# Fewer idle matmuls ahead of the first MoE unit: sixteen become four

## The chip, the core and the metric

The kernel runs on one core of one Trainium2 chip. The metric is the time of one execution on the device, in microseconds (us).

## The reference, cut to what matters

Windowed attention over 8 batches x 8 heads x 576 tokens of 64, then a two-layer feed-forward ("MoE") over the 4608 resulting tokens:

```python
scores = q @ k.T / 8                       # only |i - j| <= 32 kept
x = (softmax(scores) @ v)                  # -> 4608 x 512
h = x @ w_in                               # 512 -> 2048
out = (relu(h) ** 2) @ w_out               # 2048 -> 512
```

## The kernel before

The program is recorded as a list of operations, each with an estimated duration. A scheduler orders them per engine with a model of the chip. After that, `fill` puts idle matmuls (zeros times zeros, read by nobody) into the gaps that the model foresees on TensorE (PE) in the first 36 us, up to the first MoE unit (`self.first`), to keep the array active:

```python
WARM, COLD, DENSE, SPARSE, EXTRA = 36000, 6000, 1.15, 0.95, 6
...
def fill(self, out):
    at = 1200
    for op in sorted((o for o in out if o.eng == "PE"), key=lambda o: o.start):
        gap = min(op.start, WARM, self.first.start) - at
        one = 107 if at < COLD else 54
        for k in range(int((gap - 60) * (DENSE if at < COLD else SPARSE) // one) + (EXTRA if op is self.first else 0)):
            w = Op()
            w.eng, w.fn, w.dma, w.deps, w.i = "PE", self.idle, None, {self.idle_on}, op.i
            ...
            out.append(w)
        at = max(at, op.start + op.dur)
...
self.p.idle = lambda e: e.matmul(self.OUTP[1][:, 0:128], self.ZZ[:, 0:128], self.ZZ[:, 0:128], start=True, stop=True)
```

The MoE starts while attention of the first batch is still running, in units of 16 matmuls: 128 tokens (group g) times 512 columns of `w_in` (piece q). A unit needs its tokens' `xt` and its piece of `w_in`. The order of the first three units is (g0, q0), (g1, q0), (g0, q1), so the third unit is the first that needs the second piece:

```python
def mm1_small(self, T, g, q, key):
    ...
    first = self.p.rec("PE", f, reads=[("xt", 8*T + 2*g), ("xt", 8*T + 2*g + 1), ("w1", q)],
                       writes=[("ht", k % 2), ("mo", k)], key=key, dur=900)
    if not k:
        self.p.first = first

ORDER = ("k01 q01 v00 v01 v02 k03 q03 v03 k04 q04 w10 v04 w11 w12 w13 k05 q05 ... "   # order of the loads
         "w20 w21 w22 w23 k12 q12 v12 ...")                                            # w1x: w_in, w2x: w_out
```

The loads are issued by GpSimd (POOL), each piece of `w_in` and `w_out` is one DMA of 512 KB.

The softmax here doesn't subtract the row's maximum and nothing guards it: scores larger than these inputs give would overflow.

## Time and profile before

| | before |
|---|---|
| time, 3 executions | 300.83 us median (300.46 to 301.0) |
| profiled execution | 300.43 us, span 298.6 us |
| PE busy | 290.6 us (97%) |
| chain that ended last | 93% PE |
| first / third MoE unit starts | 18.15 / 20.65 us |
| second piece of `w_in` | issued 11.27, lands 20.27 us |

The landing is the last of the 16 increments of that DMA's semaphore in the trace. The Trainium skill ("DMA: Bandwidth & Descriptors", Why a DMA increments its semaphore by 16 and not by 1) says that each of up to 16 engines adds 1 when its own share is written, and that only the full 16 means that the data is there.

The timeline of before on PE around the first units (start, duration, engine, line, operation, count; idle time before it and its releaser in brackets, if any). The attention matmuls between are left out.

```profile
17.26 1.05 PE L411 MATMUL outp<-zz 128*128 128x128 bf16 x16
18.15 1.06 PE L787 MATMUL ht<-xt,w 128*128 128x128 bf16 x16
19.05 0.39 PE L768 MATMUL outp<-identw,xr 128*128 128x128 bf16 x4
...
19.51 1.06 PE L787 MATMUL ht<-xt,w 128*128 128x128 bf16 x16
...
20.65 1.06 PE L787 MATMUL ht<-xt,w 128*128 128x128 bf16 x16
21.84 0.40 PE L768 MATMUL outp<-identw,xr 128*128 128x128 bf16 x4
```

L411 are the idle matmuls, L787 the units, L768 transposes of the attention's result. The 16 idle matmuls hold PE for 0.89 us (18.15 - 17.26) just ahead of the first unit. The chain of before through the same stretch (start, us, what) says that they are on it:

```profile
17.42 0.89 PE outp L411 x16
18.32 0.89 PE ht L787 x16
19.21 0.22 PE outp L768 x4
...
19.68 0.89 PE ht L787 x16
...
20.85 0.22 DVE rs L750
...
21.09 0.70 DVE xr L752
```

A trap of reading: the chain counts a matmul from the modelled end of the one before it, so its times lie about 0.16 us after the starts in the timeline (17.42 against 17.26).

### The profile page before, as it was taken

How to read it: one execution, taken by the hardware profiler on the slowest of the kernel's cores; microseconds unless marked ns; L12 is line 12 of the kernel's file. 1: busy time of each engine (PE TensorE's matmuls, PEld its weight loads, DVE VectorE, ACT ScalarE, POOL GpSimd, SP SyncE). 2: the span in 40 equal slices, each digit the busy share in tenths (PEclk: the TensorE clock that was granted, in tenths of full speed). 3: DMA queues.
4: the chain of work that ended last, by engine and by line, in shares of the span. 5: the costliest groups of instructions: out<-in, count | busy, mean ns of one | idle time of the engine just before them, and what ended most of it. 6: DMA issues, size and time to landing. Idle time of an engine off the chain costs nothing.

```text
span 298.6 us, 7036 instructions
## 1 busy us (share of the span) xinstructions
PE 290.6 (97%) x2754; PEld 171.6 (57%) x2789; DVE 175.2 (59%) x428; ACT 160.1 (54%) x267; POOL 105.1 (35%) x131
## 2 busy tenths in 40 slices
PE   7899999999999999999999999999999999999996
PEld 6799855867667864544444444544544444444445
DVE  5874656674998964986569645855577622222200
ACT  3566543656667765665656454664656444444411
POOL 8999841432434444442533334334310000000000
DMA  9999999999999999999999999999992110100022
GB/s 154 168 201 170 206 173 194 159 157 190 147 179 169 121 194 154 146 143 173 145 120 136 153 163 136 116 163 141 152 124 70 55 44 35 37 35 36 35 91 86
DMA packets 166817, 39.34 MB, mean 132 GB/s; under 512 B 157824, under 2 KB 162304, under 8 KB 166784
## 3 DMA queue, kind: packets, MB, share of 16 engines
q0 software_dynamic: 113120, 17.90, 90.8%
q1 hardware_dynamic: 46512, 11.15, 25.2%
q10 hardware_dynamic: 7152, 9.83, 9.7%
q8 instruction: 22, 0.36, 0.5%
q14 instruction: 11, 0.09, 0.1%
HBM read 36.70 MB, written 9.44 MB: 155 GB/s over the span
## 4 chain that ended last, share of the span: by engine, by line
PE 93%; DMA 2%; DVE 2%; issue 1%; ACT 0%; POOL 0%; ACTq 0%; DVEq 0%; POOLq 0%
PE outp L880 40%; PE ht L828 27%; PE ht L810 7%; PE ht L787 7%; PE sc L596 4%; PE sc L664 3%; DMA qraw<-in_q_dram 2%; PE sc L490 1%; PE outp L411 1%; DVE vd L542 1%; PE sc L856 1%; PE outp L856 1%; DVE xr L752 1%; PE ht L490 0%; PE outp L768 0%
## 5 line engine op out<-in xcount | busy, mean ns | idle before, releaser
L880 PE MATMUL outp<-w,gt 128*128 128x512 bf16 x534 | 133.9, 379 | 2.0 <-issue 1.0
L843 DVE TENSOR_TENSOR gt<-rt 128x512 bf16<-128x512 bf16 x144 | 59.7, 420 | 62.8 <-ACT rt L834 53.3
L828 PE MATMUL ht<-xt,w 128*128 128x512 bf16 x375 | 95.8, 379 | 0.6 <-issue 0.2
L834 ACT ACTIVATE rt<-ht 128x512 bf16<-128x512 f32 x96 | 57.3, 599 | 68.9 <-PE ht L828 64.1
L880 PEld LDWEIGHTS outp<-w,gt 128*128 128x128 bf16 x560 | 52.4, 98 | 57.4
L828 PEld LDWEIGHTS ht<-xt,w 128*128 128x128 bf16 x384 | 36.8, 98 | 43.1
L464 POOL DMA_DIRECT2D qraw<-in_q_dram x39 | 33.4, 857 | 49.0 <-PE ht L828 13.2
L464 POOL DMA_DIRECT2D kraw<-in_k_dram x39 | 33.4, 857 | 36.2 <-PE ht L828 17.8
L530 POOL DMA_DIRECT2D vx<-in_v_dram x40 | 34.4, 862 | 29.2 <-PE ht L828 15.9
L624 ACT ACTIVATE e<-sc 128x1024 bf16<-128x1024 f32 (+1 forms) x46 | 35.7, 818 | 7.9 <-PE sc L596 7.9
L887 ACT ACTIVATE oe<-outp 128x512 f32<-128x512 f32 x35 | 20.9, 599 | 22.4 <-PE outp L880 22.4
L688 DVE TENSOR_TENSOR xr<-pf,rs 128x512 bf16<-128x512 f32 (+1 forms) x42 | 27.6, 682 | 0.4
L787 PE MATMUL ht<-xt,w 128*128 128x128 bf16 x384 | 23.8, 219 | 0.0
L810 PE MATMUL ht<-xt,w 128*128 128x256 bf16 x192 | 23.5, 273 | 0.0
L645 DVE TENSOR_TENSOR pt<-e,mask 128x512 bf16<-128x512 bf16 x42 | 17.7, 421 | 8.9 <-ACT e L624 8.8
L787 PEld LDWEIGHTS ht<-xt,w 128*128 128x128 bf16 x384 | 21.8, 98 | 0.4
L681 DVE COPY pf<-sc 128x520 f32<-128x520 f32 x21 | 14.7, 699 | 11.2 <-PE sc L664 11.1
L810 PEld LDWEIGHTS ht<-xt,w 128*128 128x128 bf16 x192 | 18.0, 98 | 3.3
L795 ACT ACTIVATE rt<-ht 128x512 bf16<-128x512 f32 x24 | 14.2, 599 | 9.3 <-PE ht L787 8.8
L816 ACT ACTIVATE rt<-ht 128x512 bf16<-128x512 f32 x24 | 14.4, 599 | 7.1 <-PE ht L810 6.0
L683 DVE TENSOR_TENSOR pf<-pf 64x520 f32<-64x520 f32 x21 | 14.6, 698 | 5.8 <-ACT pf L678 5.0
L678 ACT ACTIVATE pf<-sc 128x520 f32<-128x520 f32 x21 | 12.6, 600 | 7.2 <-PE sc L664 6.8
(81 smaller groups left out, 190.7 us busy)
## 6 DMA issues: line engine op xcount, KB each, us to landing
out_dram<-oe ACTq DMA_DIRECT2D x35, 256.0 KB, 3.1
kraw<-in_k_dram POOLq DMA_DIRECT2D x30, 128.0 KB, 5.3
qraw<-in_q_dram POOLq DMA_DIRECT2D x30, 128.0 KB, 5.6
vx<-in_v_dram POOLq DMA_DIRECT2D x24, 128.0 KB, 5.4
w<-in_moe_w_in_dram POOLq DMA_DIRECT2D x4, 512.0 KB, 9.9
w<-in_moe_w_out_dram POOLq DMA_DIRECT2D x4, 512.0 KB, 16.6
vx<-in_v_dram POOLq DMA_DIRECT2D x16, 96.0 KB, 5.0
xt<-xr SPq DMA_TRANSPOSE x36, 4.5
```

The lines of the kernel that those rows point to most:

```text
L464: self.p.rec("POOL", lambda e: e.dma_start(dst, src), writes=[("fraw", b, t, x)], old=[("fraw", b - 2, t, y + (b == 2))], reads=self.pace( ...
L530: self.p.rec("POOL", lambda e: e.dma_start(self.VX[b % 2][r:r + n, s, :, 0:64], self.v[b, :, t0:t0 + n, :].rearrange("h p d -> p h d")), w ...
L624: self.p.rec("ACT", lambda e, d=dst, a=src: e.activation(d, a, ACTF.Exp, scale=0.125), reads=["s" + x for x in name], writes=[("e", h)], k ...
L645: self.p.rec("DVE", lambda e, a=pt, c=ee, d=mb: e.tensor_tensor(a, c, d, ALU.mult), reads=[("e", k // 2), "mask"], writes=[("ptt", k)], ol ...
L688: self.p.rec("DVE", lambda e, w=w, np=np: e.tensor_tensor(bass.AP(self.XR, 512 * (2 * y + w), [[2048, np], [64, 2], [128, 4], [1, 64]]), b ...
L787: mm = e.matmul(ht[:, 128 * (d % 4):128 * (d % 4) + 128], self.W1[:, ft, 128 * d:128 * d + 128], self.XT[:, ft, t0:t0 + 128], start=(ft == ...
L810: mm = e.matmul(ht[:, 256 * (d % 2):256 * (d % 2) + 256], self.W1[:, ft, 128 * d:128 * d + 128], self.XT[:, ft, 64 * s0:64 * s0 + 256], st ...
L828: mm = e.matmul(ht[:], self.W1[:, ft, 128 * d:128 * d + 128], self.XT[:, ft, 512 * T:512 * T + 512], start=(ft == 0), stop=(ft == 3))
L834: self.p.rec("ACT", lambda e: e.activation(rt[:], ht[:], ACTF.Relu), reads=[("ht", k % 2)], writes=[("rt", k % 4)], key=key, dur=560)
L843: self.p.rec("DVE", lambda e: e.tensor_tensor(g, r, r, ALU.mult), reads=[("rt", k % 4)], writes=tags, key=key, dur=430)
L880: mm = e.matmul(op, gt[:, d, 128 * u:128 * u + 128], self.W2[:, d, :], start=(d == 0), stop=(d == 15))
L887: self.p.rec("ACT", lambda e: e.activation(oe[:], op, ACTF.Copy), reads=[tag], writes=[("oe", x % 4)], key=key, dur=560)
```

## The change

Its intent: the reserve of 6 idle matmuls ahead of the first unit goes, and the last gap is filled by 0.4 of its length instead of 0.95. Less filling, so that the first unit can start earlier when its inputs are there.

```diff
-WARM, COLD, DENSE, SPARSE, EXTRA = 36000, 6000, 1.15, 0.95, 6
+WARM, COLD, DENSE, SPARSE, LASTF = 36000, 6000, 1.15, 0.95, 0.4
@@ def fill
-            for k in range(int((gap - 60) * (DENSE if at < COLD else SPARSE) // one) + (EXTRA if op is self.first else 0)):
+            for k in range(int((gap - 60) * (DENSE if at < COLD else LASTF if op is self.first else SPARSE) // one)):
```

A comparison of the two programs' instructions engine by engine shows one difference: 16 idle matmuls ahead of the first unit became 4. DVE, ACT, POOL and SP have the same instructions in the same order.

## The prediction

> **What bounds the kernel.** TensorE's order of work. The page has PE busy 290.6 of 298.6 us (97%), and PE has 93% of the chain of work that ended last. From 17.42 us on that chain leaves PE in its first part once only, for DVE (20.85 to 21.79, a reciprocal and a scaling that feed a transpose). A shift of PE's order ahead of 22 us should reach the end, unless it runs into something that arrives at a fixed time.
>
> **What the change does.** It alters only idle matmuls (128x128, zeros) ahead of the first MoE unit. The timeline shows 16 at 17.26 to 18.15 us, start to start 55 to 56 ns. 6 are the reserve, 10 come from the 0.95 rule, so the schedule's gap less 60 ns is 568 to 625 ns, and the new rule (0.4) leaves 4. Twelve go: 12 x 55.6 = 0.67 us of PE time. No other instruction, semaphore, DMA or order changes.
>
> **How much is on the critical path.** All 16 stand in the chain. But the first unit also needs its weights: the first w_in piece, issued at 9.68 us, lands 7.7 us later, at 17.4; transposes that waited for a DMA started 0.05 us after it. Four idle matmuls end at 17.49, so the unit can start there, 0.67 us earlier, with nothing to spare. Then, from the timeline:
> - the transpose after it needs xr, which DVE ends at 18.39: start 18.44 instead of 19.05;
> - the next attention matmuls need pt (DVE, 18.72): about 18.78 instead of 19.27; second unit 19.02 instead of 19.51;
> - the third unit needs the second w_in piece, issued 11.27, 9.0 us to land: about 20.32 instead of 20.65;
> - the DVE pair and next transpose follow attention matmuls now at 19.92: transpose about 21.35 instead of 21.84.
>
> So 0.67 us shrinks to about 0.49 us by 22 us. Behind that, fixed arrivals leave room: the last w_out piece lands at 41.4 and its matmuls run at 42.05; later query and key pieces have 0.7 us and more. The shift just fits. Gain: 0.45 us.
>
> **Clock.** Idle matmuls keep the array's clock up. In the Trainium skill, "TensorE: Matmul & The Clock Gate" (Part 1), activity lifts the throttle and an idle window of about 3.4 us brings it back. The trace agrees on the first: idle matmuls step by 107 ns until 4.5 us and by 56 after. After pauses of 0.91 and 0.84 us (before 7.43 and 12.75 us) 128-column matmuls still step by 56 ns. A late weight would open a hole of at most about 0.6 us. I expect no slow matmuls.
>
> **Prediction.** 300.4 us, 299.9 to 300.9 (8 in 10). Faster by over 2%: 0.01; within 2%: 0.98; slower by over 2%: 0.01. The runs of before spread over 0.54 us, about the gain.
>
> **What would show each step.** In the timeline: 91 idle matmuls instead of 103, 4 ahead of the first unit; that unit at 17.45 to 17.6; the third at 20.2 to 20.4, waiting for w; the transpose near 21.35; PE work at 30, 60 and 250 us earlier by 0.4 to 0.5 us; first units' matmuls still 55 to 56 ns apart. If PE is early at 22 us but not at 50, a DMA absorbed it: then PE waits for w at about 41.4.
>
> **What would make it wrong.** The first weights' landing may scatter by some tenths of a us between runs; 16 idle matmuls hid that, now it shows (gain 0.2 or less). Later loads may be tighter than this trace says. Or the clock drops after the thinner stretch: units at 17 to 21 us at 107 ns per matmul, about 0.8 us more each, a loss of 1 to 3 us.

## More of the kernel before

Lines of the page of before: busy time by engine, the chain of work that ended last by engine, and two groups of matmuls (count, busy us and mean ns, idle time before them and what ended it).

```profile
PE 290.6 (97%) x2754; PEld 171.6 (57%) x2789; DVE 175.2 (59%) x428; ACT 160.1 (54%) x267; POOL 105.1 (35%) x131
PE 93%; DMA 2%; DVE 2%; issue 1%; ACT 0%; POOL 0%; ACTq 0%; DVEq 0%; POOLq 0%
L880 PE MATMUL outp<-w,gt 128*128 128x512 bf16 x534 | 133.9, 379 | 2.0 <-issue 1.0
L787 PE MATMUL ht<-xt,w 128*128 128x128 bf16 x384 | 23.8, 219 | 0.0
```

PE has almost no idle time, and the chain runs through PE's own order. The L787 group (the small MoE units) waits for nothing. The L880 group has 534 records where the program issues 560: some records are missing from this trace, so its busy time must not be compared with another trace to a few us.

## The result

| | before | changed |
|---|---|---|
| time, 4 executions each | 300.64 us median (300.40 to 301.0) | 301.09 us median (300.89 to 301.77) |
| ratio | | 1.0018 (95%: 0.9998 to 1.0038) |
| profiled execution | 300.43 us | 301.0 us |

The change did not gain 0.45 us; it measured 0.45 us over before, which is not clear of noise, and outside the predicted range of 299.9 to 300.9.

The page of the changed kernel, the lines that answer to those of before:

```profile
PE 293.9 (98%) x2777; PEld 171.6 (57%) x2777; DVE 175.4 (59%) x428; ACT 160.0 (53%) x267; POOL 105.0 (35%) x131
PE 92%; POOL 3%; DMA 3%; issue 0%; DVE 0%; POOLq 0%
L880 PE MATMUL outp<-w,gt 128*128 128x512 bf16 x560 | 138.5, 379 | 0.0
L787 PE MATMUL ht<-xt,w 128*128 128x128 bf16 x384 | 24.0, 219 | 0.9 <-DMA w<-in_moe_w_in_dram 0.9
```

PE busy rose by 3.3 us although work was taken away: that is the missing records of before (534 against 560), not a slowdown; the mean of one matmul is 379 ns in both. What is new is at the end of the last line: the small units waited 0.9 us for a DMA of `w_in`. The timeline on PE shows where:

```profile
17.32 0.39 PE L411 MATMUL outp<-zz 128*128 128x128 bf16 x4
17.54 1.06 PE L787 MATMUL ht<-xt,w 128*128 128x128 bf16 x16
18.51 0.40 PE L768 MATMUL outp<-identw,xr 128*128 128x128 bf16 x4
...
19.10 1.06 PE L787 MATMUL ht<-xt,w 128*128 128x128 bf16 x16
...
21.32 1.07 PE L787 MATMUL ht<-xt,w 128*128 128x128 bf16 x16 [0.93 <-DMA w<-in_moe_w_in_dram]
22.23 0.39 PE L768 MATMUL outp<-identw,xr 128*128 128x128 bf16 x4
```

The first unit starts 0.61 us earlier, the second 0.41 us, and the third 0.67 us *later*: it waited for the second piece of `w_in`, which landed at 21.28 us instead of 20.27. Fifteen of its 16 shares were there at 20.31. And the chain of the changed kernel no longer goes back through the idle matmuls; it starts at that DMA:

```profile
11.30 9.97 DMA w<-in_moe_w_in_dram
21.28 0.05 issue
21.32 1.07 PE ht L787 x16
22.39 0.22 PE outp L768 x4
22.61 5.39 PE ht L787 x96
```

So the two traces say: a gain of 0.6 us at the first unit and 0.4 at the second, thrown away and more by one late weight. (By the eleventh unit PE is 0.41 us behind before, and by 60 us 0.71: a second loss of 0.3 us lies at 51 to 59 us, where the trace names no wait.) They do not say whether the change made it late. That was the question for the experiments.

### The profile page after: what moved, and what is told of

Same layout as the page of the kernel before. It is cut to its first block, busy times and chain, and to the rows that moved or that the text cites. A ratio compares the mean times of both kernels' runs of the same rounds, so it can differ in the third digit from the quotient of the medians.

```text
span 299.2 us, 7047 instructions
## 1 busy us (share of the span) xinstructions
PE 293.9 (98%) x2777; PEld 171.6 (57%) x2777; DVE 175.4 (59%) x428; ACT 160.0 (53%) x267; POOL 105.0 (35%) x131
## 4 chain that ended last, share of the span: by engine, by line
PE 92%; POOL 3%; DMA 3%; issue 0%; DVE 0%; POOLq 0%
PE outp L880 41%; PE ht L828 28%; PE ht L810 7%; PE ht L787 7%; PE sc L664 3%; DMA w<-in_moe_w_in_dram 3%; PE sc L596 3%; POOL vx L530 1%; POOL kraw L464 1%; PE sc L490 1%; POOL qraw L464 1%; PE sc L856 1%; PE outp L856 1%; PE sc L712 0%; POOL w L547 0%
## 5 line engine op out<-in xcount | busy, mean ns | idle before, releaser
L880 PE MATMUL outp<-w,gt 128*128 128x512 bf16 x560 | 138.5, 379 | 0.0
L828 PE MATMUL ht<-xt,w 128*128 128x512 bf16 x384 | 97.0, 379 | 0.0
L880 PEld LDWEIGHTS outp<-w,gt 128*128 128x128 bf16 x560 | 52.3, 98 | 57.5
```

The lines of the kernel that those rows point to most:

```text
L828: mm = e.matmul(ht[:], self.W1[:, ft, 128 * d:128 * d + 128], self.XT[:, ft, 512 * T:512 * T + 512], start=(ft == 0), stop=(ft == 3))
L880: mm = e.matmul(op, gt[:, d, 128 * u:128 * u + 128], self.W2[:, d, :], start=(d == 0), stop=(d == 15))
```

## The experiments

Every job ran its kernels on one chip (not the same one in every job), together with the kernel before as a standing reference (two executions of it in each round). All runs gave correct results. Unless said otherwise an edit is to the number of idle matmuls in one gap, made with this (the key is the start of the operation behind the gap in the scheduler's model; 16924 is the first unit, 20186 the third):

```diff
-            for k in range(int((gap - 60) * (...) // one)):
+            for k in range(max(0, int((gap - 60) * (...) // one)) + MORE.get(round(op.start), 0)):
```

In the first two jobs `max` was not there yet, or stood around the whole sum; it matters only for gaps behind the first unit.

### First job: is it the instruction count?

The changed kernel has 24 instructions of PE less (12 matmuls, 12 weight loads). PE's instructions come by DMA too: the traces show 22 packets of 16 KB on one queue of kind "instruction", of 0.9 to 1 us each early in the kernel. The Trainium skill ("Runtime: NRT & Kernel Launch", Instruction fetch mechanics) has refills of 16 KiB, 256 instructions each, and calls their cost mostly hidden. The traces agree on the size: 22 times 256 is 5632, and before has 5578 matmuls and weight loads of PE. One theory was that fewer instructions move these fetches against the weights; the rival was plain scatter.

The changed kernel again, unedited:

> The changed kernel again, for five rounds and a second trace. In the first trace the third MoE unit started at 21.32 us, waiting for the second w_in piece, which landed at 21.28 (before: 20.27); one of its 16 shares came 0.98 us after the 15th. Theory S (scatter: that late share is chance, whatever the kernel): the piece lands anywhere in 20.2 to 21.3 in this trace, and the time is within 0.2 us of before, at most 0.3 us faster. Theory F (fetch: 24 fewer instructions of TensorE move its instruction fetches against this piece, and a fetch of 16 KB, 0.94 us, sits in front of the late share every time): the piece lands at 21.1 to 21.4 again and the kernel is 0.3 to 0.6 us slower than before.

Measured: 301.44 us median of 6 (300.14 to 303.00), ratio to the reference 1.0032 (1.0007 to 1.0058). Piece at 21.25, third unit at 21.30. It looked like theory F, except that one execution of 300.14 beat everything seen so far.

```diff
+MORE = {11539: 12}
```

> The changed kernel with 12 idle matmuls put into the hole of 1.0 us before the transpose at 12.75 us, where TensorE waits for DVE anyway, so that TensorE's instruction count ahead of the MoE units is that of before, while the first unit still starts at about 17.5. Theory F: the second w_in piece lands at 20.2 to 20.4 as before, third unit at about 20.3, time 0.3 to 0.5 us less than before. Theory S: same time as the changed kernel within 0.2 us.

Measured: 300.35 us median of 5 (300.33 to 300.83), ratio 0.9999. Piece at 20.70, third unit at 20.75. Neither theory's number: better than the changed kernel, but not 0.3 us under before.

```diff
+MORE = {16924: 12, 15382: -11, 14184: -1}
```

> All 16 idle matmuls ahead of the first unit, as before, but 12 others left out (11 at 15.7 us, where TensorE waits for DVE anyway, and one at 14.9), so that the instruction count is that of the changed kernel with the first unit still at about 18.15. Theory F: the second w_in piece is late (21.1 to 21.4) and the time is that of the changed kernel, 0.3 to 0.6 us over before. Theory S: time of before within 0.2 us.

Measured: 300.67 us median of 6 (300.34 to 301.51), ratio 1.0005. Undecided. Its profile fell on an execution of 301.28 us in which the first unit already started at 19.06, because of copies on DVE before 11.5 us (below), so the fetch came at another time than planned. The piece landed at 20.40.

```diff
-GT0, WT0 = (12.5, 16, 20, 25.5), (13, 18, 23, 26)
+GT0, WT0 = (12.5, 16, 20, 25.5), (13, 20.5, 23, 26)
```

> The changed kernel with another MoE unit third: one that needs the first w_in piece, landed since 17.3, and the third pair of token chunks, so that the second w_in piece is needed a unit later (about 21 us or after). The scheduler moves a few instructions at 36 to 47 us with it. Both theories say that the wait of 0.9 us at 21.3 goes or shrinks to 0.3 us, TensorE is 0.4 to 0.9 us ahead of the changed kernel from 22 us on, and the time is 0.4 to 0.9 us less than the changed kernel's. If the time does not fall, the wait for this piece is not what cost the gain.

Measured: 300.46 us median of 6 (300.17 to 301.46), ratio 1.000. The third unit now started at 20.22 with no wait, while the piece again landed at 21.28; the eleventh unit started at 28.27 against 29.45 in the changed kernel's first trace. That overstates the lead, because the edit also puts transposes and attention matmuls behind units. Where the two orders coincide again, at 46.8 us, PE is 0.55 us ahead of the changed kernel's first trace, so the wait for this piece is a real cost of that trace. Over before the lead there is 0.13 us, and a wait for a DMA transpose (0.19 us at 85.4) took the rest.

### Second job: a race with a fetch?

In three traces with 4 idle matmuls and no padding (changed, rep_after, other_unit), the DMA packets show the second fetch at 19.23 to 19.26 us, when the last semaphore writes of that piece were still to come. That made a sharp theory, easily tested by moving the fetch by tenths of a us.

```diff
+MORE = {15382: -6}
```

> New theory R (race of a fetch with a share): of five traces, three (all with 4 idle matmuls and no padding) have TensorE's second 16 KB instruction fetch at 19.23 to 19.26 us on a DMA engine that had not yet written the semaphore of its share of the second w_in piece; that write then comes at 20.2 to 20.4 and takes effect at 21.25 to 21.28. In the trace of before the same fetch starts at 19.27, 10 ns after its engine's write at 19.26, and the piece lands at 20.27. Here the changed kernel has 6 idle matmuls (12 instructions of TensorE) less at 15.7 us, where TensorE waits for DVE, so the fetch should come about 0.3 us later, at 19.4 to 19.7. R: after every write that it can delay, so the piece lands at 20.2 to 20.7, third unit at 20.3 to 20.7, median 300.0 to 300.4, below the changed kernel by 0.5 us or more. S (chance, whatever the instructions): times spread as the changed kernel's, 300.1 to 303, median about 301.

Measured: 301.24 us median of 6 (300.71 to 303.08), ratio 1.0026. The fetch moved to 19.91; the piece came at 20.75 and the third unit at 20.89, nearly as forecast, and yet the time did not fall. In its profile PE's starts slip by 0.72 us at 86 us, waiting for a DMA transpose of `xt`.

```diff
+MORE = {16924: 12, 11539: 3}
```

> The kernel before with 3 idle matmuls more in the hole at 12 us, where TensorE waits for DVE; the fetch should come about 0.15 us earlier, at 19.1, ahead of its engine's semaphore write at 19.26. R: the second w_in piece lands at 20.7 to 21.3, the third unit starts at 20.75 to 21.35 and the median is 300.7 to 301.1, 0.3 to 0.5 us over before, by 3 idle matmuls that fill nothing but a wait. S: time of before within 0.15 us.

Measured: 300.82 us median of 5 (300.48 to 300.87), ratio 1.0004. The median fits theory R, the trace does not: fetch at 19.14 as planned, piece at 20.24, not late (that execution took 300.48 us). **As a forecast theory R fell here**: a fetch ahead of the write need not make the piece late. A later trace of the changed kernel (s4_after, below) has the fetch at 19.24 and the piece at 20.57. What of the theory survives stands below, after the table of landings.

```diff
-        self.p.idle = lambda e: e.matmul(self.OUTP[1][:, 0:128], self.ZZ[:, 0:128], self.ZZ[:, 0:128], ...)
+        self.p.idle = lambda e: e.matmul(self.OUTP[1][:], self.ZZ[:, 0:128], bass.AP(self.ZZ, 0, [[128, 128], [0, 4], [1, 128]]), ...)
@@ fill: (n + 1) // 4 of them where n narrow ones stood
```

> The changed kernel with idle matmuls of 512 columns, a quarter as many (20 instead of 91, 142 instructions less), for about the same time on the array. R: the fetch comes about 3 us later, past the second w_in piece, which lands at 20.2 to 20.5; third unit at about 20.3 to 20.5; median 299.9 to 300.3 and no run over 300.8. S: spread and median of the changed kernel.

Measured: 300.77 us median of 5 (300.06 to 300.91). Fetch at 22.37, out of the way; piece at 20.59, third unit at 20.72. Expected median and upper bound missed, although 300.06 is the fastest execution of the whole study.

> As the run before it, but with 4 wide idle matmuls (16 of the old) ahead of the first unit instead of 1. R: piece lands at 20.2 to 20.5, but the third unit starts at about 20.65 as in the kernel before; median 300.3 to 300.5, so that 4 against 16 is worth 0.2 to 0.4 us where the fetch is out of the way. S: time of before; no difference between this and the run before it that is larger than 0.2 us unless the third unit's start tells it.

Measured (same edit, with `MORE = {16924: 12}`): 301.11 us median of 5 (300.88 to 301.50). Piece at 20.64, third unit at 20.77. Its expectation missed by 0.7 us, with nothing early to blame: 0.72 us went at 110.6 us. Two kernels without any fetch near the piece, and still 20.6 instead of 20.3.

### Third job: the control that was missing

Four kernels, of which the last is the kernel before, character for character.

```diff
+MORE = {16924: 0}    # the 4 idle matmuls of the last gap, with 512 columns each
```

> The kernel before with its 16 narrow idle matmuls ahead of the first unit made 4 wide ones (512 columns): the same time on the array (0.86 against 0.89 us), so the first unit still starts at about 18.1, but 24 instructions of TensorE less from there on, exactly the count of the changed kernel. It separates time from instruction count. Theory F2 (the count moves every later fetch of TensorE's instructions[...], and the kernel before is lucky in where they fall): a wider spread than before, some of the runs at 301 or over, median 300.6 to 301.3. Theory T (it is the earlier start itself that costs, by bringing TensorE to waits): median 300.4, all but one run under 301.

Measured: 301.22 us median of 6 (300.67 to 302.68), ratio 1.0022; piece at 22.08 in an execution of 301.67, in which the first unit started at 18.89 instead of the expected 18.1.

```diff
+MORE = {20186: 12}
```

> The changed kernel with 12 idle matmuls just ahead of the third unit, where it waits for the second w_in piece: the first two units early as in the changed kernel, the count restored from the third unit on. The early part can lose as in the changed kernel (third unit at 20.8 if the piece lands by then, 21.3 if a fetch hits it), the later part is that of before. F2: two clusters, 300.5 and 300.8 to 301.0, nothing over 301.2. T: the spread of the changed kernel, with runs at 301.5 to 303.

Measured: 301.19 us median of 6 (300.88 to 302.16), ratio 1.0020; piece at 20.60, third unit at 21.92, because the first unit was late already (18.56).

```diff
+MORE = {16924: 12, 20186: 3}    # the 3 of 512 columns
```

> The kernel before with 3 wide idle matmuls (0.65 us, 6 instructions) ahead of the third unit, to measure what its start is worth: it moves from 20.65 to about 21.3, the start that it had in the changed kernel. If TensorE's order passes it on one to one, as the prediction supposed, the median is 301.0 (300.9 to 301.1), and the late landings of the piece (up to 21.28) no longer show, so there is one cluster instead of two. If the delay is absorbed later, 300.4 to 300.7.

Measured: 301.29 us median of 6 (300.83 to 302.29), ratio 1.0024. The median is above both forecasts. In its trace the third unit started at 21.42, 0.77 us after before's, and the eleventh at 29.54, 0.50 us after before's 29.04; no part of that 0.50 was given back up to 179 us.

> The kernel before against itself, for a second trace and for the spread: ratio 1.000 within 0.001; two clusters at about 300.4 and 300.85 (of its 26 runs so far 17 lie at 300.36 to 300.48 and 7 at 300.75 to 300.92). Its trace has the second w_in piece at 20.3 if the run is of the lower cluster, at 20.9 to 21.3 and the third unit with it if it is of the upper one.

Measured: **301.41 us median of 6 (300.86 to 302.78), ratio of the kernel before to itself 1.0031, 95% interval 1.0011 to 1.0051.** Its profile fell on the slowest, 302.78 us, with the piece at 20.40: not the piece, then, made that one slow. This run overturns the reading of all the others. An identical text was as far from the reference as the changed kernel was. So neither "1.0018" nor "1.0032" of the changed kernel can be put down to the change, and the medians of single runs above can't be ordered by less than about 1 us.

### Fourth and fifth job: like against like

> First of four places in one job: the changed kernel. The control of the last job showed the kernel before at 301.41 us median when it was submitted as an experiment, against 300.46 for the same text as the standing reference of the job, so that all comparisons with that reference carry an offset of up to 0.95 us that is not the kernel's. Here both kernels are submitted twice as experiments (changed, before, before, changed). Theory P (place and scatter): each of the four has a median of 300.4 to 301.6 and the two kernels' pooled medians of 10 to 12 runs lie within 0.4 us of each other. Theory K (the change costs time): both copies of the changed kernel are 0.4 us or more over both copies of before.

> Second place: the kernel before. P: median 300.9 to 301.6, as its copy in the last job, though its text is the reference's; K: median 300.4 to 300.6.

> Third place: the kernel before again. As the second place; how far the two differ tells what two copies of one text differ by. P: they may differ by as much as either differs from the changed kernel.

> Fourth place: the changed kernel again. P: within 0.5 us of the first place. In its trace, as in that of the first place: first unit at 17.5 to 17.7 if nothing ahead of it is late, third unit 0.05 us after the second w_in piece lands, wherever that is in 20.2 to 22.1.

> The kernel before once more, now in the first place of a job, where the changed kernel was in the last one. In that job the two copies of the changed kernel had medians of 300.33 and 301.63, the two of before 300.39 and 300.62. P (place and scatter): median anywhere in 300.4 to 301.6, fastest run 300.36 to 300.5.

> The changed kernel in the second place. P: median anywhere in 300.2 to 301.6, fastest run 300.1 to 300.3 (about 0.2 us under the fastest of before, which is what the traces without a late piece say the change is worth). K (the change costs time): median 0.4 us or more over that of the other kernel of this job.

Measured, all copies of the two texts:

| job | copy | text | median (range), executions | the job's reference |
|---|---|---|---|---|
| 1 | rep_after | changed | 301.44 (300.14 to 303.00), 6 | 300.45 |
| 3 | rep_before | before | 301.41 (300.86 to 302.78), 6 | 300.46 |
| 4 | s1_after | changed | 300.33 (300.19 to 301.96), 6 | 300.85 |
| 4 | s2_before | before | 300.39 (300.38 to 300.80), 5 | 300.85 |
| 4 | s3_before | before | 300.62 (300.52 to 301.54), 5 | 300.85 |
| 4 | s4_after | changed | 301.63 (300.79 to 304.53), 6 | 300.85 |
| 5 | s5_before | before | 301.25 (300.84 to 302.67), 6 | 300.46 |
| 5 | s6_after | changed | 300.88 (300.28 to 300.96), 6 | 300.46 |

Two copies of the changed kernel in one job differ by 1.30 us; four copies of before, in three jobs, by up to 1.02 us. Pooled, the changed kernel has a median of 300.91 (mean 301.26, 24 executions), before 301.00 (mean 301.14, 22 executions). The difference of the means is +0.12 us with a standard error of 0.26 us if the executions are taken as independent. They are not, since copies differ: with the mean of a copy as the unit, four against four, it is +0.16 with a standard error of 0.38. Executions over 301.5 us: 9 of 24 against 6 of 22. Theory K (both copies of the changed kernel in one job 0.4 us or more over both of before) is refuted by s1_after. Theory P missed its numbers too: in the fourth job the pooled medians are 301.25 (changed) and 300.53 (before), 0.73 us apart where it allowed 0.4; s4_after is 1.30 us from s1_after where it allowed 0.5; s2_before and s3_before lie below its 300.9, and the fastest of s5_before (300.84) lies above its 300.5. What stands is weaker: two copies of one text differ by more than the two kernels do, and neither a gain of 0.45 us nor a loss of some tenths is excluded by these times. The traces, next, say more.

### What the traces of these copies show

The timeline lines of the third unit, the transpose and the fourth unit, in s1_after (an execution of 300.21 us):

```profile
20.63 1.05 PE L787 MATMUL ht<-xt,w 128*128 128x128 bf16 x16 [0.17 <-DMA w<-in_moe_w_in_dram]
21.52 0.39 PE L768 MATMUL outp<-identw,xr 128*128 128x128 bf16 x4
21.75 1.06 PE L787 MATMUL ht<-xt,w 128*128 128x128 bf16 x16
```

and in s2_before (300.80 us):

```profile
21.36 1.05 PE L787 MATMUL ht<-xt,w 128*128 128x128 bf16 x16 [0.49 <-ACT rt L795]
22.25 0.39 PE L768 MATMUL outp<-identw,xr 128*128 128x128 bf16 x4
```

In the second the kernel *before* has the late piece: it landed at 21.22 us. (The releaser named, an activation of ACT at 20.67 to 21.27, belongs to the second unit and is not an input of the third. The piece is.) With the first traces and the other copies this makes a table of kernel against landing (s3_before, late already at its first unit, is left out):

| trace | piece lands | third unit | fourth unit | eleventh unit | that execution |
|---|---|---|---|---|---|
| before | 20.27 | 20.65 | 22.07 | 29.04 | 300.43 |
| rep_before | 20.40 | 20.70 | 22.13 | 29.21 | 302.78 |
| s5_before | 19.98 | 20.70 | 22.13 | 29.20 | 301.15 |
| s2_before | 21.22 | 21.36 | 22.47 | 29.44 | 300.80 |
| s1_after | 20.50 | 20.63 | 21.75 | 28.75 | 300.21 |
| s4_after | 20.57 | 20.62 | 21.75 | 28.75 | 301.98 |
| changed | 21.28 | 21.32 | 22.45 | 29.45 | 301.0 |
| rep_after | 21.25 | 21.30 | 22.43 | 29.43 | 300.80 |
| s6_after | 21.28 | 21.42 | 22.53 | 29.50 | 300.96 |

When the piece is late, both kernels start the eleventh unit at 29.43 to 29.50: the time saved before it is waited away, and the change is worth nothing. When it comes early, the changed kernel is 0.29 us ahead of the first trace of before there (0.45 of the two other copies), by the fourth unit's earlier transposes more than by the third unit.

The late traces have one thing in common. The traces also hold each DMA packet, among them the 4-byte writes by which an engine reports its share. In all six traces with a late piece (the four of the table, other_unit with 21.28 and before_w4 with 22.08) one of the last of these writes begins at the end of PE's second instruction fetch, from 0.02 us before it to 0.17 us after it, and takes 24 to 73 ns; the semaphore's last step follows 0.9 to 1.1 us later. In the 14 other traces the last write takes 22 ns and its step follows after 0.3 to 0.4 us. So the lateness goes with a fetch just ahead of one share's write, in both kernels. It is an order in time and not a proof: the kept traces do not say on which DMA engine a packet ran, and a fetch at that time is not enough (of the ten traces with the fetch at 19.14 to 19.27 us, five are late).

Even then not all arrives. The timeline of s1_after around 41 us:

```profile
41.35 0.41 PE L664 MATMUL sc<-vx,pt 128*128 128x65 bf16 x8
41.75 1.90 PE L880 MATMUL outp<-w,gt 128*128 128x512 bf16 x8
```

and of before:

```profile
41.65 0.41 PE L664 MATMUL sc<-vx,pt 128*128 128x65 bf16 x8
41.89 1.89 PE L880 MATMUL outp<-w,gt 128*128 128x512 bf16 x8
```

From the L664 group to L880 it is 0.40 us in s1_after and 0.24 in before: the last piece of `w_out` landed at 41.70 us, and PE, ahead of before by 0.30, had to wait 0.15 us for it. From 60 us on PE's starts are only 0.09 us ahead of before (0.10 in s4_after, up to its wait at 87 us), and the last matmul starts at 295.87 against 295.97 us. The spans end at 298.4 and 298.6 us; half of that difference lies behind the last matmul. So an undisturbed execution gains at most 0.2 us, and the fastest executions agree: 300.14, 300.19 and 300.21 of the copies of the changed kernel against 300.38, 300.39 and 300.39 of before.

The slow executions, over 301.5 us, are of both kernels. The longest waits of PE in rep_before (302.78 us), and the line of its timeline where it falls:

```profile
PE ht L810 <- DMA xt<-xr: 1.6, 1, 1.6
87.78 1.05 PE L810 MATMUL ht<-xt,w 128*128 128x256 bf16 x8 [1.63 <-DMA xt<-xr]
```

and the same two of s4_after (301.98 us):

```profile
PE ht L810 <- DMA xt<-xr: 1.6, 1, 1.6
87.01 1.05 PE L810 MATMUL ht<-xt,w 128*128 128x256 bf16 x8 [1.60 <-DMA xt<-xr]
```

One kind of loss, then, at one place in the program in both profiles: a unit whose tokens come by a DMA transpose, which in rep_before was issued at 79.35 and landed at 87.74 us, and in the first trace of before at 77.81 and 84.91. A second kind lies on DVE before the first unit. The three copies of values before 11 us in s3_before (301.54 us):

```profile
9.20 2.19 DVE L542 COPY vd<-vx 64x528 bf16<-64x528 bf16 x3
```

and in before:

```profile
9.42 1.19 DVE L542 COPY vd<-vx 64x528 bf16<-64x528 bf16 x3
```

The same copies take 1.0 us longer (in cut_early too, 2.21 us), and in s3_before the first unit starts at 19.23 us instead of 18.15, with its 16 idle matmuls unchanged. The Trainium skill ("SBUF — State Buffer", SBUF: two separate sides) says that DVE, in some modes, and GpSimd hold a shared port exclusively, the loser waiting; POOL issues DMAs all through this stretch, so it would fit, but no run here isolates it.

## Why the prediction was wrong

- **"Twelve go", 4 stay:** right. The programs differ in 16 against 4, and the traces have 103 and 91 idle matmuls.
- **"The unit can start there" (17.49, 0.67 us earlier):** right. 17.54 in the first trace, 17.49 to 17.61 in the four copies.
- **The transpose after it at 18.44, second unit at 19.02:** right within 0.1 us (18.51 and 19.10).
- **"The third unit needs the second w_in piece, issued 11.27, 9.0 us to land: about 20.32 instead of 20.65":** this step failed. It took one landing of one trace as a fixed arrival. In 20 traces the piece lands at 19.98 to 22.08 us, median 20.62, so 20.27 was on the early side. In the five traces of the changed kernel it landed at 20.50, 20.57, 21.25, 21.28 and 21.28, and the third unit started at 20.62 to 21.42. The prediction named the scatter of the *first* weights as a risk; those landed at 17.27 to 17.55 in all five, and cost 0.1 us at most (rep_after, first unit at 17.59). The second ones did it. In the first trace of the changed kernel that turned a lead of 0.41 us at the second unit into a lag of 0.41 us at the eleventh.
- **"The shift just fits" behind 22 us:** wrong by the wait of 0.15 us for the last `w_out` piece in s1_after. That piece landed at 41.70 us there, 0.29 us later than in before: again one landing (41.17 to 42.18 us in 20 traces) was taken as fixed. The room was also put at 0.6 us by setting a time of the chain (42.05) against a landing (41.4). By the timeline the matmuls of before started at 41.89: the room is 0.48 us.
- **"Gain: 0.45 us":** mis-sized. At most 0.2 us where the piece comes early, of which 0.1 us is seen at PE's last matmul, and none where it comes late.
- **"A shift of PE's order ahead of 22 us should reach the end":** right for what is left after 22 us. In delay_third the third unit started 0.77 us later than in before and the fourth 0.47 us later; the eleventh was 0.50 us later, and that stayed up to 179 us.
- **Clock:** right. The first unit's matmuls still step by 55 to 57 ns in the changed kernel's trace, behind 4 idle matmuls, and in s6_after the units after the third one's wait are as long as before.
- **The range, 299.9 to 300.9:** too narrow, for a reason that the prediction had in hand and used wrongly. "The runs of before spread over 0.54 us" came from three executions. Four copies of before, 22 executions, spread over 2.40 us (300.38 to 302.78), with medians from 300.39 to 301.41. The measured 301.09 is well inside what the kernel before itself gives.

What stays open. Why a copy submitted as an experiment has a pooled median of 301.00 us where the same text as the standing reference has 300.46 (55 executions in five jobs) was not found; two of the four copies of before, in the fourth job, were no worse than their reference. Whether the earlier start makes the late landing more frequent is open too: 3 of 5 traces of the changed kernel are late against 1 of 5 of before, too few to say. And what lets a fetch meet a share's write in one execution and not in another is not known. The forecasts made from the fetch theory missed in both runs that tested it: the time of after_minus6 (301.24 us for 300.0 to 300.4) and the landing of before_plus3 (20.24 us for 20.7 to 21.3).

## What to carry to other kernels

A trace gives one draw of each DMA's landing. Before a gain is counted that ends in a wait for a DMA, look at the spread of that landing in several traces, and at the margins behind it by starts in the timeline, not by times of the chain. And measure a change of a few tenths of a us against a copy of the old kernel that is submitted in the same way; without that control the study would have explained a slowdown that the runs do not show.

## What the Trainium skill lacked or had wrong

- "TensorE: Matmul & The Clock Gate" (Part 1) has the change to the full clock at around 4 us of activity, give or take 500 ns from run to run, and elsewhere warns that it varies. Here the idle matmuls start at 1.0 us in each trace, and the last step of 107 ns ends between 3.63 us (rep_before) and 6.93 us (rep_after) in 18 traces: a spread of 3.3 us, where 500 ns to either side is 1.0 us. (The two other traces have idle matmuls of 512 columns.)
- "DMA: Bandwidth & Descriptors" (Why a DMA increments its semaphore by 16 and not by 1) explains the 16 shares, but not how far the last one can be behind on loaded queues. For the second `w_in` piece the 16th came 0.97 us after the 15th in the changed kernel's trace and 0.31 us after it in before's (19.95 and 20.27). No page says either that a share can be late behind a fetch of instructions: here, in six traces, the semaphore's step came 0.9 to 1.1 us after a write that began at the end of a fetch, instead of 0.3 to 0.4 us.
- No page used says how far two copies of one program differ on one chip: here medians of 300.39 and 300.62 us (before) and of 300.33 and 301.63 us (changed) in one job.
